# Moving pair 1's state products ahead of a weight tile, and thirteen small matmuls in place of one filler, in an SSD and PReLU kernel on TensorE

## The chip, the cores and the metric

The kernel runs on one core of one Trainium2 chip. The metric is the device time in microseconds (us) of one execution. Times inside an execution are counted from the start of the span, which runs from the first to the last instruction that the profile shows.

## The reference

Two stages follow each other. The first is a state-space recurrence (Mamba 2) over 4 batches, 8 heads, 768 positions, head dimension 32 and state size 16, by chunks:

```python
cum = np.cumsum(la, axis=-1)
L = np.exp(cum[:, :, :, None] - cum[:, :, None, :]) * causal
M = np.einsum('bhin,bhjn->bhij', Cc, Bc) * L
y_intra = np.einsum('bhij,bhjd->bhid', M, xc)
y_inter = np.einsum('bhin,bhnd->bhid', Cc, state) * decay_to_i[:, :, :, None]
y[:, :, sl] = y_intra + y_inter
state = decay_full[:, :, None, None] * state + np.sum(Bx, axis=2)
```

Its result, as 3072 tokens of 256 values, goes through a layer of 2048 hidden units with a PReLU of one slope per unit:

```python
h = x @ w_in                                   # 256 -> 2048
g = np.maximum(h, 0.0) + alpha * np.minimum(h, 0.0)
out = g @ w_out                                # 2048 -> 256
```

The two weights arrive as float64 and are made into float32 in the kernel.

## The kernel before, in words

**Staging.** The 3072 tokens are 24 chunks of 128, handled in pairs of chunks. Six groups of 512 tokens (two pairs each) go through the layer. For group 0 the layer is written out plainly: `hidden` (L1077) multiplies a 128-column piece of w_in with the group's 512 tokens, ScalarE (L1080) and VectorE (L1081) do the PReLU, and `output` (L1124) multiplies the result with a piece of w_out into four PSUM banks. Later groups use a scheme of seven products for eight (L1198, L1208, L1223, L1280) and take most of the time. The recurrence for a later pair is done in advance, in pieces between these products.

**Order.** Nothing is scheduled at run time: the order of the code is the order of the instructions on each engine. Each of TensorE, VectorE, ScalarE, GpSimd and SyncE (which issues the transfers) goes through its own list and waits for tiles by semaphores. PSUM is held in pools: `ss` and `hp` (two tiles each) and four `bank`s.

**Weights.** Pieces of 512 columns come as raw float64 halves (transfers issued at L254) and are turned to float32 by hand on three engines: ScalarE L270, L280 and L283, VectorE L293 and L305, GpSimd (or VectorE) L275, and last GpSimd L327, which adds the two parts into `w_in` or `w_out`. A matmul with such a piece waits for L327.

**The first two pairs.** `first_two` does pairs 0 and 1 by halves of 64 positions, and between the steps multiplies the first tokens with the first pieces of w_in (`hidden_two`: two pieces of w_in, each in two steps k, 256 tokens, PSUM tile handed in; matmuls at L1092). For one pair, the steps are:
- `turned`: transposes of B and C on TensorE (L838), copied out by ScalarE (L840)
- `spread`: 32 small matmuls (L858) that copy decays over partitions; VectorE scans them (L864)
- `spread_c`: ScalarE makes `cz` (L847)
- `added`: 16 matmuls of 64 x 32 tiles (L888), the chunks' additions to the state; `states` (L903, VectorE, three and then one) chains them; `one_at_a_time` masks the states on GpSimd (L909)
- `gram_of`: 16 matmuls (L874), and `times` (L880, VectorE) multiplies them with the scanned decays
- `x_products`: 32 matmuls (L922) and `state_products` (L934), which sum the output of the pair; ScalarE copies it out (L942, L943)

The change touches a filler behind `spread` of pair 1 and the place of `added` of pair 1. In the kernel before, `hidden_two` for the third and fourth piece of w_in is called with `among(i, k)`, which runs after each of its four matmuls: `added`, `states` and `one_at_a_time` after the first, `gram_of`, `times`, the last state and a PReLU after the second, and `x_products`, `state_products` and `copy_out` after the third.

**Fillers.** `keep_warm(to, n, cols)` (L331 to L336) multiplies a constant tile of ones with itself into a PSUM tile that is not yet needed; its result is read by nobody. It stands at several places of the first part.

**Later pairs.** From pair 2 on, `pair` does the same steps with full chunks (L624 the state products, L637 the states on VectorE, L562 the scans, L737 the gram, L748 its product with the decays). The decay factors that L637 needs come by two transfers: `pf<-rpf` (L442) writes them out, `ap<-pf` (L167) brings them back spread over the partitions.

Of the kernel before, what the change touches and what calls it, by code (L numbers as in the profile page):

```python
# [22 lines left out]
def kernel(  # L23
# [25 lines left out]
    nc = tc.nc  # L49
# [7 lines left out]
    Q = 128  # L57
# [46 lines left out]
    def bank(i):  # L104


        return ps_q.tile([P, 512], F32, name="bank", tag=f"q{i}")
# [180 lines left out]
    def sign(dst, src, sg):  # L288

        if src.dtype == F32 or id(dst) in signs:  # L290
            return
        r = wtp.tile([P, 2, WQ], U32, name="wr")
        nc.vector.tensor_single_scalar(out=r, in_=parts[id(dst)][0], scalar=SIGN,  # L293
                                       op=ALU.bitwise_and)
        signs[id(dst)] = r
# [34 lines left out]
    warm = nc.const_aps.tensor(1.0, [P, 1], F32)  # L330

    def keep_warm(to, n, cols=2 * Q):

        for i in range(n):
            nc.tensor.matmul(to[:, :cols], warm.to_broadcast([P, P]), warm.to_broadcast([P, cols]),
                             start=True, stop=True, skip_group_check=True)  # L336
# [53 lines left out]
    def slope_signs():  # L390
        if moe_w_out.dtype == F32:
            nc.vector.tensor_single_scalar(out=s_out, in_=s_mul.bitcast(U32), scalar=SIGN,
                                           op=ALU.bitwise_and)
        else:
            for o, by in ((g_mul, 2.0**-11), (g_add, 2.0**25)):
                nc.gpsimd.tensor_scalar(out=o, in0=s_mul, scalar1=by, scalar2=None, op0=ALU.mult)
# [119 lines left out]
    def pair_loads(gp):  # L516

        b, c = divmod(2 * gp, CPB)
        nat, abc, xt, ap = loads["p", gp]

        bn = work.tile([P, 2, H * N], F32, name="bn")
        i, bi = divmod(b, 2)
        if gp >= HALF:
            pj = prt[i].rearrange("p (j b m h) -> p j b m h", j=2, b=2, h=H)[:, :, bi, c // 2]
        else:
            pj = (prt[i if gp >= NB else "short"]
                  .rearrange("p (b h c) -> p b c h", b=2, h=H)[:, bi, c : c + 2])
        nc.gpsimd.tensor_tensor(
            out=bn.rearrange("p k (h n) -> p k h n", h=H),
            in0=nat[:, 0].rearrange("p k (h n) -> p k h n", h=H),  # L530
            in1=pj.unsqueeze(3).to_broadcast([P, 2, H, N]), op=ALU.mult)
        return bn
# [8 lines left out]
    def spare():  # L541

        return ps_h.tile([P, GT], F32, name="hp", tag="hp")
# [272 lines left out]
    def first_two():  # L816
# [34 lines left out]
        def spread(z, ts):  # L851
            for e in range(2):
                for r in range(4):
                    rs = slice(32 * r, 32 * r + 32)
                    row = 32 * r + N * e
                    for j, hs in enumerate(halves):
                        o = ts[r][hs, : 2 * Q].rearrange("p (k e t) -> p k e t", k=2, e=2)
                        nc.tensor.matmul(o[:, :, e], ident[rs, row : row + 1]  # L858
                                         .to_broadcast([32, HQ]), z[rs, :, hs], start=e == 0,
                                         stop=True, tile_position=(32 * r, HQ * j),  # L860
                                         skip_group_check=True)
# [5 lines left out]
        def gram_of(bc, cz, banks):  # L867
            for v in range(2):
                for k in range(2):
                    for r in (2 * v, 2 * v + 1):  # L870
                        rs = slice(32 * r, 32 * r + 32)
                        for j, hs in enumerate(halves):
                            o = banks[r][hs, (2 + k) * Q : (3 + k) * Q]
                            nc.tensor.matmul(o.rearrange("p (e t) -> p e t", e=2), bc[rs, k, hs],  # L874
                                             cz[rs, :, k, hs], start=True, stop=True,
                                             tile_position=(32 * r, HQ * j),
                                             skip_group_check=True)

        def times(i, r, t):
            nc.vector.tensor_tensor(out=dec[i][:, r], in0=t[:, 2 * Q :], in1=dec[i][:, r],  # L880
                                    op=ALU.mult)

        def added(dps, bn, xt):
            for k in range(2):
                for r in range(4):
                    rs = slice(32 * r, 32 * r + 32)
                    for j, hs in enumerate(halves):
                        nc.tensor.matmul(dps[j][rs, k], bn[hs, k, rs],  # L888
                                         xt[hs, k, 2 * r * D : 2 * (r + 1) * D],
                                         start=True, stop=True, tile_position=(HQ * j, 32 * r),  # L890
                                         skip_group_check=True)

        def dps_in(banks):
            return [t[:, 2 * Q : 2 * Q + 4 * D].rearrange("p (k m) -> p k m", k=2) for t in banks]

        def states(i, dps, pf, cs=range(4)):
            for c in cs:
                if i == 0 and c == 0:
                    nc.scalar.copy(out=new[0][:, 0], in_=dps[0][:, 0])
                    continue  # L900
                e = (c + 1) * HQ - 1
                old = new[i][:, c - 1] if c else new[0][:, 3]
                nc.vector.scalar_tensor_tensor(out=new[i][:, c], in0=old, scalar=pf[:, e : e + 1],  # L903
                                               in1=dps[c % 2][:, c // 2], op0=ALU.mult,
                                               op1=ALU.add)

        def mask(i, cs):
            n = cs.stop - cs.start
            nc.gpsimd.tensor_tensor(  # L909
                out=sm[i][:, cs].rearrange("p k (g m) -> p k g m", g=2),  # L910
                in0=new[i][:, cs].unsqueeze(2).to_broadcast([P, n, 2, 2 * D]),
                in1=hmask.rearrange("p (g m) -> p g m", g=2).unsqueeze(1)
                .to_broadcast([P, n, 2, 2 * D]), op=ALU.mult)
# [31 lines left out]
        def places(first, second):  # L945
            return [[t[:, :Q].rearrange("p (k t) -> p k t", k=2) for t in ts]
                    for ts in (first, second)]
# [4 lines left out]
        def decayed_c(bc, pf):  # L952
            cd = work.tile([P, 2, Q], F32, name="cd")
            nc.gpsimd.tensor_tensor(out=cd.rearrange("p k t -> p (k t)"),
                                    in0=bc[:, 2:].rearrange("p k t -> p (k t)"), in1=pf,
                                    op=ALU.mult)
            return cd

        def one_at_a_time(i, cs):
            for c in cs:  # L960
                mask(i, slice(c, c + 1))
# [9 lines left out]
        sp = [bank(r) for r in range(4)]  # L971
# [5 lines left out]
        nat1, _, xt1, pf1 = loads["p", 1]  # L977
# [13 lines left out]
        dps = dps_in([hp, tp])  # L991
# [18 lines left out]
        sp = [bank(r) for r in range(4)]  # L1010
# [1 line left out]
        x_products(y, xt0, 0, (1,))  # L1012
        state_products(y, 0, cd0)
        spread(z1, sp)
        keep_warm(sp[3][:, 2 * Q :], 1)
        convert_next(halves=(nc.gpsimd, nc.gpsimd))
        xts[0] = xtp.tile([P, KC, GT], F32, name="xT")
        copy_out(0, y)
# [8 lines left out]
        bn1 = pair_loads(1)  # L1027
        convert_next(first=False)
        own = [ss(), ss()]
        second = spare()  # L1030
        bc1 = turned(nat1, (own[0], second))
        cz1 = spread_c(bc1)
        dps = dps_in(own)
        mask(0, slice(3, 4))
        slope_signs()
        cd1 = decayed_c(bc1, pf1)

        def among(i, k):
            if (i, k) == (0, 0):
                added(dps, bn1, xt1)  # L1040
                states(1, dps, pf1, range(3))
                one_at_a_time(1, range(3))
            if (i, k) == (0, 1):
                gram_of(bc1, cz1, sp)
                for r in range(4):
                    times(1, r, sp[r])
                states(1, dps, pf1, (3,))
                prelu_of[0]()
                convert_a(*pieces[2])
                sign(*pieces[2])  # L1050
            if (i, k) == (1, 0):
                y = places([own[0], bank(0)], [bank(1), bank(2)])
                x_products(y, xt1, 1)
                state_products(y, 1, cd1)
                copy_out(1, y)
# [349 lines left out]
    def convert_next(first=True, **kw):  # L1405


        i = done[0]
        if i < len(pieces):
            convert(*pieces[i], **kw)  # L1410
            if first and i and i + 2 < len(pieces):
                convert_a(*pieces[i + 2])
            if loaded[0] == i + 6:
                load_next()
        done[0] += 1
# [147 lines left out]
```

## Time and profile before

| what | value |
|---|---|
| times of three runs | 361.19, 361.89, 363.96 us (median 361.89) |
| the profiled execution's own time | 361.22 us |
| its span, from first to last instruction | 359.5 us |
| mean granted TensorE clock | 0.991 |
| instructions | 7769, of them 2981 matmuls and 2981 weight loads |
| half clock granted | up to 6.47 us, and from 23.54 to 30.36 us |
| VectorE, ScalarE, GpSimd busy | 67%, 48%, 56% of the span |
| data moved | 30.24 MB, mean 84 GB/s |

The span leaves out 1.7 us that lie before the first and after the last instruction. A float32 matmul stands in the trace as two passes with a weight load each, so a call of `nc.tensor.matmul` counts two in PE and two in PEld; a transpose counts one. In the timeline lines the columns are: start (us), length (us), engine, line, operation, what it writes and reads, the tile of the array, the shape, and how often it follows in a row; in brackets the idle time before it and what released it. The page also gives the share of 16 DMA engines that are moving data.

### The profile page before, as it was taken

How to read it: one execution, taken by the hardware profiler on the slowest of the kernel's cores; microseconds unless marked ns; L12 is line 12 of the kernel's file. 1: busy time of each engine (PE TensorE's matmuls, PEld its weight loads, DVE VectorE, ACT ScalarE, POOL GpSimd, SP SyncE). 2: the span in 40 equal slices, each digit the busy share in tenths (PEclk: the TensorE clock that was granted, in tenths of full speed). 3: DMA queues.
4: the chain of work that ended last, by engine and by line, in shares of the span. 5: the costliest groups of instructions: out<-in, count | busy, mean ns of one | idle time of the engine just before them, and what ended most of it. 6: DMA issues, size and time to landing. Idle time of an engine off the chain costs nothing.

```text
span 359.5 us, 7769 instructions
## 1 busy us (share of the span) xinstructions
PE 352.6 (98%) x2981; PEld 286.4 (80%) x2981; DVE 239.6 (67%) x483; ACT 172.3 (48%) x391; POOL 202.2 (56%) x227
## 2 busy tenths in 40 slices
PE   8889999999999999999999999999999999999996
PEld 3567566668888888888888888888888888888885
DVE  6966996999947856866656856657856634643363
ACT  3537666535354445445345445445545444443431
POOL 6653748579847947536546536537536545434510
PEclk9988999999999999999999999999999999999999
DMA  8999999205436502502522521531201001001102
GB/s 149 189 211 339 253 282 204 77 2 116 131 86 145 110 3 60 116 3 49 101 61 51 94 64 43 97 69 42 34 2 31 0 2 29 2 1 29 33 0 58
DMA packets 105581, 30.24 MB, mean 84 GB/s; under 512 B 79896, under 2 KB 101448, under 8 KB 105544
## 3 DMA queue, kind: packets, MB, share of 16 engines
q1 hardware_dynamic: 103048, 29.43, 35.6%
q10 hardware_dynamic: 2496, 0.32, 0.6%
q8 instruction: 23, 0.38, 0.4%
q14 instruction: 14, 0.11, 0.1%
HBM read 26.32 MB, written 3.42 MB: 83 GB/s over the span
## 4 chain that ended last, share of the span: by engine, by line
PE 96%; DMA 1%; DVE 1%; issue 0%; POOL 0%; SPq 0%; ACT 0%; POOLq 0%
PE bank L1198 33%; PE hp L1223 28%; PE bank L1124 8%; PE hp L1077 6%; PE ss L1223 6%; PE hp L1092 2%; PE ss L782 1%; PE ss L726 1%; DMA nat<-in_B_dram 1%; PE bank L1191 1%; PE ss L800 1%; PE ss L774 1%; PE ss L737 1%; PE bank L1092 1%; PE ss L613 1%; PE ss L934 0%
## 5 line engine op out<-in xcount | busy, mean ns | idle before, releaser
L1280 POOL TENSOR_TENSOR gt<-gt 128x512 f32<-128x512 f32 x58 | 74.2, 1278 | 21.1 <-DVE gt L1208 16.3
L1198 PE MATMUL bank<-gt,w_out 128*128 128x256 f32 x320 | 83.5, 381 | 0.0
L1198 PEld LDWEIGHTS bank<-gt,w_out 128*128 128x128 f32 x320 | 60.1, 190 | 9.2 <-issue 1.0
L1208 DVE SCALAR_TENSOR_TENSOR gt<-hp,s_mul,gt 128x256 f32<-128x256 f32 x96 | 42.0, 479 | 29.1 <-ACT gt L1206 26.8
L1270 POOL TENSOR_TENSOR gt<-gt 128x512 f32<-128x512 f32 x20 | 25.4, 1269 | 62.6 <-DVE gt L1208 49.8
L1206 ACT ACTIVATE gt<-hp,s_alpha 128x256 f32<-128x256 f32 x96 | 40.3, 471 | 34.6 <-PE hp L1223 31.5
L1198 PE MATMUL bank<-gt,ws 128*128 128x256 f32 x224 | 55.9, 379 | 0.0
L1198 PEld LDWEIGHTS bank<-gt,ws 128*128 128x128 f32 x224 | 42.3, 190 | 5.6
L1223 PE MATMUL hp<-xs,w_in 128*128 128x256 f32 x160 | 41.9, 384 | 0.0
L1223 PE MATMUL hp<-xs,ws 128*128 128x256 f32 x160 | 41.2, 380 | 0.0
L1249 DVE TENSOR_TENSOR hp<-hp,u 128x512 f32<-128x512 f32 x20 | 14.0, 700 | 35.2 <-ACT u L1247 35.2
L1223 PEld LDWEIGHTS hp<-xs,ws 128*128 128x128 f32 x160 | 30.3, 190 | 4.3 <-POOL xs L1165 0.2
L1223 PEld LDWEIGHTS hp<-xs,w_in 128*128 128x128 f32 x160 | 29.7, 190 | 4.5
L1124 PE MATMUL bank<-w_out,gt 128*128 128x256 f32 x128 | 31.0, 384 | 0.0
L1124 PEld LDWEIGHTS bank<-w_out,gt 128*128 128x128 f32 x128 | 23.6, 190 | 6.5 <-issue 2.9
L1223 PE MATMUL ss<-xT,w_in 128*128 128x256 f32 x96 | 24.6, 379 | 0.0
L1077 PE MATMUL hp<-xT,w_in 128*128 128x512 f32 x48 | 22.7, 595 | 0.0
L556 DVE TENSOR_TENSOR_SCAN dec<-abc,bank 128x192 f32<-128x192 f32 x48 | 22.7, 523 | 0.0
L640 POOL TENSOR_TENSOR sm<-state,bmask 128x256 f32<-128x256 f32 (+1 forms) x10 | 6.2, 619 | 28.9 <-DVE state L637 28.9
L1238 ACT COPY m<-hp 128x512 f32<-128x512 f32 x8 | 4.7, 586 | 35.7 <-PE hp L1223 35.7
L1247 ACT COPY u<-hp 128x512 f32<-128x512 f32 x20 | 11.7, 585 | 19.4 <-PE hp L1223 19.4
L1208 DVE SCALAR_TENSOR_TENSOR gt<-c,s_mul,gt 128x256 f32<-128x256 f32 x40 | 20.6, 555 | 0.0
(230 smaller groups left out, 615.8 us busy)
## 6 DMA issues: line engine op xcount, KB each, us to landing
abc<-z SPq DMA_DIRECT2D x24, 192.0 KB
raw<-in_moe_w_in_dram SPq DMA_DIRECT2D x8, 512.0 KB
raw<-in_moe_w_out_dram SPq DMA_DIRECT2D x8, 512.0 KB
abc<-z SPq DMA_DIRECT2D x8, 512.0 KB
out_dram<-o_sb SPq DMA_DIRECT2D x32, 64.0 KB
nat<-in_B_dram SPq DMA_DIRECT2D x26, 64.0 KB
xt<-in_x_dram SPq DMA_DIRECT2D x12, 128.0 KB
xt<-in_x_dram SPq DMA_DIRECT2D x24, 64.0 KB
```

What stands on the lines that cost most here:

```text
L556: nc.vector.tensor_tensor_scan(out=dv[:, o : o + SQ], data0=abc[k][:, s : s + SQ], data1=ident_p[0][:, :SQ], initial=0.0, op0=ALU.mult, op ...
L1077: nc.tensor.matmul(hp, w_in[:, k, f * P : (f + 1) * P], xts[g][:, k], start=(k == 0), stop=(k == KC - 1))
L1092: nc.tensor.matmul(hp[:, i * nt : (i + 1) * nt], w_in[:, k, fs], xts[g][:, k, ts], start=(i == 0 and k == 0), stop=(k == KC - 1), skip_gro ...
L1124: nc.tensor.matmul(pos[0][t // 2][:, t % 2], gt[:, t * Q : (t + 1) * Q], w_out[:, f], start=(f == 0 and t % 2 == 0), stop=(f == NF - 1), s ...
L1198: nc.tensor.matmul(ms[g][i][:, h], w, blocks[g, z][n][:, p], start=(q == 0 and h == 0), stop=(q == NQ - 1), skip_group_check=True)
L1206: nc.scalar.mul(o[:, p], h[:, p], s_alpha[:, fs[p]])
L1208: nc.vector.scalar_tensor_tensor(out=o[:, p], in0=h[:, p], scalar=s_mul[:, fs[p]], in1=o[:, p], op0=ALU.mult, op1=ALU.max)
L1223: nc.tensor.matmul(to[:, p], w(2 * z + p), b, start=start and p == 0, stop=True, skip_group_check=True)
L1247: nc.scalar.copy(out=u2, in_=A)
L1249: nc.vector.tensor_tensor(out=Y, in0=Y, in1=u2, op=ALU.add)
L1270: nc.gpsimd.tensor_tensor(out=tc_, in0=g22, in1=g12, op=ALU.subtract)
L1280: eng.tensor_tensor(out=o, in0=x0, in1=x1, op=ALU.subtract)
```

## The change

It has two parts.

1. Behind `spread` of pair 1, the filler of one matmul of 128 x 128 with 256 columns is replaced by thirteen matmuls of 32 x 32 with 32 columns, of the same constant, on the corner tile of the array (position 0, 0), into the same PSUM bank.
2. `added`, `states` and `one_at_a_time` of pair 1 leave `among(0, 0)` and are issued in front of the call of `hidden_two` for the third piece of w_in; behind them comes a new filler of 256 columns into `second`, the PSUM tile that this `hidden_two` is about to use.

```diff
         spread(z1, sp)
-        keep_warm(sp[3][:, 2 * Q :], 1)
+        small = sp[3][:32, 2 * Q : 2 * Q + 32]
+        for i in range(13):
+            nc.tensor.matmul(small, warm[:32].to_broadcast([32, 32]),
+                             warm[:32].to_broadcast([32, 32]), start=True, stop=True,
+                             tile_position=(0, 0), skip_group_check=True)
         convert_next(halves=(nc.gpsimd, nc.gpsimd))
...
         cd1 = decayed_c(bc1, pf1)
+        added(dps, bn1, xt1)
+        states(1, dps, pf1, range(3))
+        one_at_a_time(1, range(3))
+        keep_warm(second, 1)
 
         def among(i, k):
-            if (i, k) == (0, 0):
-                added(dps, bn1, xt1)
-                states(1, dps, pf1, range(3))
-                one_at_a_time(1, range(3))
             if (i, k) == (0, 1):
                 gram_of(bc1, cz1, sp)
```

On VectorE, ScalarE, GpSimd and SyncE the instructions keep their order; only TensorE's list changes. Lines behind the change are four further on in the kernel after (L1092 becomes L1096, L1077 becomes L1081, L1081 becomes L1085, L1124 becomes L1128).

## The prediction

> **What bounds the kernel now.** I began with the page's busy times and its chain of work, then read the windows view in steps of 3.41 us (the rhythm of the granted clock), TensorE's timeline around the edit, and last VectorE, GpSimd and the transfers up to 50 us.
>
> ```profile
> PE 352.6 (98%) x2981; PEld 286.4 (80%) x2981; DVE 239.6 (67%) x483; ACT 172.3 (48%) x391; POOL 202.2 (56%) x227
> PE 96%; DMA 1%; DVE 1%; issue 0%; POOL 0%; SPq 0%; ACT 0%; POOLq 0%
> q8 instruction: 23, 0.38, 0.4%
> ```
>
> TensorE is the bound: 352.6 of 359.5 us. Only its few holes, or time at a reduced clock, can be won. Its last two holes lie where the edit is made:
>
> ```profile
> 13.37 0.70 PE L335 MATMUL bank<-const-float32-1.0 128*128 128x256 f32 x2
> ...
> 17.87 0.70 PE L1092 MATMUL hp<-xT,w_in 128*128 128x256 f32 x2 [1.20 <-POOL w_in L327]
> 18.50 0.46 PE L888 MATMUL ss<-xt,bn 64*32 64x64 f32 x32
> 18.89 0.70 PE L1092 MATMUL hp<-xT,w_in 128*128 128x256 f32 x2
> 19.52 0.72 PE L874 MATMUL bank<-cz,bc 32*64 32x128 f32 x32
> ...
> 23.05 0.41 PE L922 MATMUL bank<-dec,xt 64*32 64x64 f32 x20 [1.05 <-issue]
> ...
> 25.19 0.79 PE L1092 MATMUL hp<-xT,w_in 128*128 128x256 f32 x1
> ```
>
> The reader should see two holes: 1.20 us for the third tile of w_in, which GpSimd finishes at 17.82, and 1.05 us in the middle of the x_products, released by nothing but "issue". The second I read as instructions not yet there. Matmul and weight load count 2 x 2981 = 5962 instructions, and queue q8 has 23 packets: some 260 each. The stall falls inside a row of equal matmuls that wait for nothing. In the packet records one such packet moves at 20.58-21.63, behind data on full queues, and TensorE goes on 1.4 us after it.
>
> ```profile
> 16.70:20.11 3.41, 2.24 (x68) 1.36 (x68) 2.31 (x6) 2.96 (x8) 3.28 (x7) 1.00 1.01 314
> 20.11:23.53 3.42, 2.35 (x79) 1.41 (x70) 3.21 (x9) 0.47 (x1) 1.28 (x3) 1.00 0.85 105
> 23.53:26.94 3.41, 3.41 (x20) 3.02 (x21) 1.98 (x4) 1.36 (x6) 1.92 (x2) 0.50 1.04 253
> 26.94:30.35 3.41, 3.41 (x9) 2.69 (x9) 2.19 (x4) 2.41 (x6) 1.19 (x2) 0.50 0.92 293
> ```
>
> Columns: stretch, length, busy time of PE, PEld, DVE, ACT, POOL, the granted clock, the DMA share, GB/s. After the window of 20.11, full of tiny matmuls and holding the hole, the clock is halved for two windows: 6.83 us, in which 3.41 us of work is lost. From 25.19 on TensorE has no hole to the end.
>
> **What the Trainium skill says.** "Runtime: NRT & Kernel Launch", section Instruction fetch mechanics: the sequencer fetches blocks of 256 instructions by its own DMA queue, a cost it calls "mostly hidden". The trace agrees on the block (23 packets) and disagrees once on hidden (1.05 us). "TensorE: Matmul & The Clock Gate", Part 1: activity in a free-running window of 3413 ns releases the throttle, an idle window restores it. The trace shows the steps (23.54 to 30.36 is 2 x 3.41), but here a window with 2.35 of 3.42 us marked busy was followed by half speed, so what counts must be use of the array, not "busy".
>
> **The change part by part.** Each matmul stands in the trace as two passes with two weight loads.
> 1. Out: one filler of 256 columns, 13.37 to 13.98: 0.61. In: 13 x 2 passes of 32 x 32. Nearest row: passes of 64 columns on one tile (L922) every 56 ns. Half that for half the columns, or no less than that: 26 x 28 = 0.73 to 26 x 56 = 1.46. I take 0.75, so +0.14 (range +0.1 to +0.85). What follows, L1092 at 13.98, stops for GpSimd's L327, which ends at 14.62, then come the transposes L838 and the 1.20 hole: 0.14 is free. At +0.85 up to 0.45 would reach the copies of ScalarE (L840, 17.08 and 17.35) that free the PSUM for added.
> 2. Count: 12 more matmuls here, one filler more later: 13 x 4 = 52 more instructions ahead of the x_products (48 by the first L1092 of the third tile). They draw the request for the next block forward, from between 14.4 and 16.4, when the DMA share is 1.00, to about 13, where the packet records are at 0.14-0.38. Then it is there well before 21.
> 3. Added products (L888, 16 matmuls, 32 passes) before the third tile. They wait for xt (landing 16.24 and 17.07), bn, and ScalarE's second copy (17.35): 17.38 + 0.39 = 17.77. That is inside the hole of 1.20. The filler takes 2 x 0.2135 = 0.43: 18.20. The four passes of L1092 take 0.85 and 0.2 for the turn of the tiling: 19.25 for the gram (19.52 before), so -0.25. No DMA, VectorE, ScalarE or GpSimd instruction changes its place in a queue; VectorE's states (L903, 19.13 to 20.11) get their operand 1.1 earlier, with scans before them to 18.17.
> 4. x_products start 0.25 earlier and lose the 1.05 hole: last one ends 22.1 for 23.46; state_products at full clock take 1.0 for 1.80: 23.1 at most and 22.5 at best for the next L1092 (25.19 before), -2.1 to -2.7.
> 5. The clock. The window from 20.11 now holds some 1 us of full-array L1092 more at its end (22.5 to 23.53), and in the window before it the filler. I take it that it stays up: +3.41 of work. Together up to 2.1 + 3.41 = 5.5 us ahead by 30.36; the low end is 1.2 (hole and order alone).
>
> That lead does not last, which is the main step. VectorE waits at 39.26 for a transfer that TensorE does not drive:
>
> ```profile
> 34.01 0.60 SPq L167 DMA_DIRECT2D ap<-pf  x1
> ```
> ```profile
> 39.26 0.28 DVE L637 SCALAR_TENSOR_TENSOR state<-gt,ap,ss 128x64 f32<-128x64 f32 x1 [0.16 <-DMA ap<-pf]
> 39.46 2.41 DVE L562 TENSOR_TENSOR_SCAN dec<-abc,bank 128x256 f32<-128x256 f32 x4
> ...
> 47.29 0.69 DVE L305 SCALAR_TENSOR_TENSOR wr<-wt,wr 128x512 uint32<-128x512 uint32 x1
> ```
> ```profile
> 48.07 1.27 POOL L327 TENSOR_TENSOR w_out<-wr,wg 128x512 uint32<-128x512 uint32 x1 [1.16 <-DVE wr L305]
> ```
> ```profile
> 49.48 0.39 PE L1124 MATMUL bank<-w_out,gt 128*128 128x256 f32 x1
> ```
>
> ap is issued at 34.01 because pf lands at 34.00 after its issue at 27.00, behind weight tiles in queues at a share near or above 1.0 from 22 on; it lands at 39.17. Behind L637 VectorE works without a hole to 47.98 (scans, two conversions, two activations), GpSimd sums the third piece of w_out from 48.07 to 49.34, and TensorE's L1124 needs that at 49.48. Slack: 0.14. However early TensorE is at 39, it starts that L1124 at 49.34 or later, and from there to the end it is full. So the gain is at most 0.14, or some 0.5 if the transfers begin a little earlier (the share of 0.85 in the window of 20.11 leaves 0.15 x 3.42 = 0.5).
>
> What is late next: TensorE, 4 to 5 us ahead, reaches pair 2's gram (L737) near 39.2 and waits for VectorE's L1081, which ends at 43.65. It stands idle about 4.4 us across the window 40.60-44.01 (the 3.41 grid continued). If the clock is halved at 44.01, the rest up to 49.48, 4.5 us of full-speed work after 43.65 (gram 1.1, two L1124 and L1077 3.5), does not fit: 43.65 to 44.01 does 0.36, the window to 47.43 1.7, the remaining 2.4 ends at 49.87 if the clock comes back: +0.4. With a second half window: 1.7 by 50.84, then 0.7 more, against 47.43 + 2.4: 51.55, so +2.1; part of it is given back where the lead is smaller. Sum for the likeliest case, against the profiled 361.22: -0.1 for the slack, +0.4 for one late half window, weighed with none: 361.2 to 361.6. The median of three runs is 361.89, 0.67 above the profiled run, so the next median may lie there too. I take 361.6.
>
> **The rivals.**
> A (likeliest, 0.57): the holes and most of the early half speed go, the lead is given back at ap; 361.2 to 362.0.
> B (0.24): the change doesn't do what it says: the stall moves to other instructions or the clock is halved all the same. For: how full a window must be is seen here in one case only, and a window a little more or less full decides. TensorE then still meets the wait at 49.34 with what it had: 361.0 to 361.9, no change either.
> C, slower (0.13): the idle stretch at 39 to 44 halves the clock for two windows or more at 44.01 and VectorE, waiting for late products, carries it on: 361.22 + 2.1 = 363.3, with both windows fully at half 361.22 + 3.4 = 364.6, and past 365.5 only with a third. It decides from a lead of about 3.4 us, which empties a whole window. For: at 23.53 the clock was halved after a window less empty than this one, and for two windows. Against: the windows before and after this one are full, unlike then.
> D, faster (0.06): ap is not the wall, because pf or the weight tiles come earlier: 361.2 - 4.9 = 356.3, half kept 358.8. Against: the slack of 0.14 is read directly.
>
> **How the numbers follow.** A and B are both within 1% (3.6 us, about what a measurement of this kernel can tell from no change: 358.3 to 365.5), most of C too. Faster: 0.05 from D. Slower: 0.05 from C's end and from the small tiles costing more than bounded. Same 0.90. Range: A and B reach 361.0 to 362.0, C to 363.8, D's partial gain to 360.5: 360.5 to 363.8.
>
> **What would show it.** No "issue" in front of L922 and x_products starting near 20.5 (steps 2, 3); windows 23.53 and 26.94 at 1.00 (step 5); L1077's first run near 26 to 27; ap landing within 0.5 of 39.17; a TensorE hole of 4 us released by VectorE before the gram L737; L1124 of the third piece within 0.2 of 49.34, or later with a clock of 0.50 from 44.01 (C). Wrong, if ap lands over 1 us earlier, if TensorE keeps a lead past 50, or if clock steps appear after 50.

## The result, and the profile after

The changed kernel took 362.90 us (median of 20 runs, 361.34 to 369.42), the kernel before 362.17 us (20 runs, 360.26 to 364.23): ratio 1.0021, 95% interval 0.9997 to 1.0045. An execution more than 1.5% above the fastest of its kernel, such as the one of 369.42, is left out of this ratio and of those below. That is no difference that this measurement can tell, or a small loss. The forecast was 361.6 (range 360.5 to 363.8) and no change.

The profiled execution of the changed kernel took 362.82 us, its span 361.1. From its page, the busy times and the chain by engine:

```profile
PE 352.7 (98%) x3007; PEld 287.9 (80%) x3007; DVE 238.3 (66%) x483; ACT 172.0 (48%) x391; POOL 202.9 (56%) x227
PE 91%; DMA 5%; DVE 3%; issue 1%; SPq 0%; ACT 0%; DVEq 0%
```

TensorE's work is the same, but the chain that ends last no longer runs over TensorE alone: 5% of it are now transfers and 3% VectorE. The chain between 25 and 53 us names them (start, length, what):

```profile
27.99 7.70 DMA pf<-rpf
35.70 0.02 issue
35.71 4.62 DMA ap<-pf
...
40.42 0.28 DVE state L637
40.70 2.33 DVE dec L562 x4
```

TensorE's timeline, and VectorE's and GpSimd's at the same place:

```profile
13.31 0.27 PE L1017 MATMUL bank<-const-float32-1.0 32*32 32x32 f32 x3
14.34 0.95 PE L1017 MATMUL bank<-const-float32-1.0 32*32 32x32 f32 x23 [0.75 <-issue]
...
20.03 0.46 PE L888 MATMUL ss<-xt,bn 64*32 64x64 f32 x32 [0.78 <-issue]
20.41 0.70 PE L335 MATMUL hp<-const-float32-1.0 128*128 128x256 f32 x2
...
44.86 0.48 PE L737 MATMUL hp<-cz,bc 32*128 32x256 f32 x1 [1.55 <-DVE gt L1085]
...
51.11 1.24 PE L1128 MATMUL bank<-w_out,gt 128*128 128x256 f32 x5
```
```profile
40.42 0.28 DVE L637 SCALAR_TENSOR_TENSOR state<-gt,ap,ss 128x64 f32<-128x64 f32 x1 [3.40 <-DMA ap<-pf]
```
```profile
48.99 1.27 POOL L327 TENSOR_TENSOR w_out<-wr,wg 128x512 uint32<-128x512 uint32 x1 [2.04 <-DVE wr L305]
```

Before, VectorE waited 0.16 us for ap; now it waits 3.40: TensorE's lead, turned into idle time of VectorE, and later into 1.55 us of TensorE's own in front of pair 2's gram. ap came 1.16 us later than before (L637 at 40.42 for 39.26), because its source was late: L439, which VectorE runs behind products of TensorE, before and after:

```profile
24.14 1.42 DVE L439 TENSOR_TENSOR_SCAN rpf<-r,zeros 96x128 f32<-96x128 f32 x1
```
```profile
26.53 1.43 DVE L439 TENSOR_TENSOR_SCAN rpf<-r,zeros 96x128 f32<-96x128 f32 x1
```

The windows view, on the 3.41 us grid of this execution (columns as before):

```profile
11.65:15.07 3.42, 2.67 (x94) 2.23 (x90) 3.14 (x8) 1.95 (x6) 2.12 (x3) 1.00 0.70 77
15.07:18.48 3.41, 3.41 (x14) 2.72 (x12) 2.86 (x5) 0.00 (x0) 2.24 (x5) 0.50 0.96 235
...
42.38:45.79 3.41, 1.86 (x17) 0.99 (x16) 3.31 (x7) 1.80 (x3) 1.65 (x3) 1.00 0.77 125
45.79:49.20 3.41, 3.41 (x9) 2.58 (x9) 3.31 (x7) 0.00 (x0) 1.29 (x3) 0.50 1.06 190
```

Two windows are at half speed, but others than before: one behind the hole in the small matmuls, one behind the idle time at the gram. The steps of the clock lie at other times too: before at 23.54, here at 15.07, and 8.47 between them is no multiple of 3.41. The grid has its own phase in each execution.

The sum of this execution: GpSimd begins the third piece of w_out 0.92 later (L327 at 48.99 for 48.07). TensorE, behind the half window, uses it only 0.85 after it is ready (ready at 50.26, used at 51.11); before that was 0.14. 0.92 + 0.85 - 0.14 = 1.63. The span grew by 1.6.

### The profile page after: what moved, and what is told of

It reads as the page before. It is cut to its first block, busy times and chain, and to the rows that moved or that the text cites. A ratio compares the mean times of both kernels' runs of the same rounds, so it can differ in the third digit from the quotient of the medians.

```text
span 361.1 us, 7820 instructions
## 1 busy us (share of the span) xinstructions
PE 352.7 (98%) x3007; PEld 287.9 (80%) x3007; DVE 238.3 (66%) x483; ACT 172.0 (48%) x391; POOL 202.9 (56%) x227
## 3 DMA queue, kind: packets, MB, share of 16 engines
HBM read 26.32 MB, written 3.42 MB: 82 GB/s over the span
## 4 chain that ended last, share of the span: by engine, by line
PE 91%; DMA 5%; DVE 3%; issue 1%; SPq 0%; ACT 0%; DVEq 0%
PE bank L1202 33%; PE hp L1227 28%; PE bank L1128 7%; PE ss L1227 6%; PE hp L1081 4%; DMA pf<-rpf 2%; PE ss L782 1%; DMA ap<-pf 1%; PE ss L726 1%; PE hp L1096 1%; DMA nat<-in_B_dram 1%; PE bank L1195 1%; PE ss L800 1%; PE ss L774 1%; PE ss L737 1%; DVE dec L562 1%
## 5 line engine op out<-in xcount | busy, mean ns | idle before, releaser
L1210 ACT ACTIVATE gt<-hp,s_alpha 128x256 f32<-128x256 f32 x96 | 40.3, 471 | 34.6 <-PE hp L1227 31.5
L1128 PE MATMUL bank<-w_out,gt 128*128 128x256 f32 x128 | 32.6, 399 | 0.0
L1128 PEld LDWEIGHTS bank<-w_out,gt 128*128 128x128 f32 x128 | 24.8, 199 | 6.8 <-issue 3.7
L1081 PE MATMUL hp<-xT,w_in 128*128 128x512 f32 x48 | 22.6, 594 | 0.0
```

The costliest lines, as they stand in the source:

```text
L1081: nc.tensor.matmul(hp, w_in[:, k, f * P : (f + 1) * P], xts[g][:, k], start=(k == 0), stop=(k == KC - 1))
L1128: nc.tensor.matmul(pos[0][t // 2][:, t % 2], gt[:, t * Q : (t + 1) * Q], w_out[:, f], start=(f == 0 and t % 2 == 0), stop=(f == NF - 1), s ...
L1210: nc.scalar.mul(o[:, p], h[:, p], s_alpha[:, fs[p]])
```

## The experiments

All times are medians over 14 to 22 runs beside the kernel before on the same chip. Where a kernel has fillers or small matmuls more or less than the changed one, only products that nobody reads are concerned.

**The parts alone, both together, and the idle time filled.** The small matmuls without the move:

```diff
-        keep_warm(sp[3][:, 2 * Q :], 1)
+        small = sp[3][:32, 2 * Q : 2 * Q + 32]
+        for i in range(13):
+            nc.tensor.matmul(small, ...)
```

> Only the thirteen small matmuls; the added products stay behind the first matmul of the third tile. Theory 1 (the wall: what TensorE does before 40 counts only where it delays VectorE's L439 and so pf and ap; a hole of instructions in the small matmuls empties the clock window there and a half clock at about 15 makes everything late): the hole of 0.7 to 0.9 us stands inside the small matmuls, half speed in one window near 15 to 18.5 where the phase is as in the profile after, ap lands 0.5 to 1.1 us later than 39.17, and the time is 0 to 1 us over before. Theory 2 (the moved products are what costs): time as before within 0.2 us. Theory 3 (fetch of instructions decides: the hole at the x_products goes, and 1 us is won): 1 us under before.

Measured: 361.80, ratio 0.9999 (0.9979 to 1.0020). That is theory 2's time, and the lower end of theory 1's. Theory 1's hole and half window did not come: in the profile the small matmuls have no hole, but the one at the x_products is there, 1.45 us, and no window after 5.3 us is at half speed. But for the hole that execution is what the forecast wanted for TensorE, and it took 360.95 us: 0.27 less than the profiled one of before, which lost 3.41 us of work at half speed. The lead is gone at L637, in VectorE's timeline:

```profile
39.14 0.28 DVE L637 SCALAR_TENSOR_TENSOR state<-gt,ap,ss 128x64 f32<-128x64 f32 x1 [3.57 <-DMA ap<-pf]
```

The move without the small matmuls:

```diff
-        for i in range(13):
-            nc.tensor.matmul(small, ...)
+        keep_warm(sp[3][:, 2 * Q :], 1)
```

> Only the move of the added products with its filler; the filler of 256 columns stays behind spread. Theory 1: no hole of instructions behind spread, the added products run inside the wait for w_in near 17.4, the x_products begin near 20.5; the hole of 1.05 us in front of the x_products stays nearly where it was, since only 4 more instructions come first; TensorE is up to 0.5 us earlier at 30 and this is given back at the wait for ap; time as before within 0.3 us. Theory 2 (the move costs): 0.4 to 0.8 us over before. Theory 3: as before, since the hole stays.

Measured: 362.07, ratio 0.9992 (0.9970 to 1.0013). Its profile has the hole at the x_products at 1.62 us and one half window from 25.06. Theory 1's time holds, and theory 2's loss did not come; theory 1's 17.4 for the added products does not hold (18.11): TensorE had waited 0.54 and 0.21 us for pieces of w_in in front of the transposes.

The filler kept in front of the small matmuls, with the move:

```diff
+        keep_warm(sp[3][:, 2 * Q :], 1)
         for i in range(13):
             nc.tensor.matmul(small, ...)
```

> The kernel after with the filler of 256 columns kept in front of the thirteen small matmuls. Theory 1: the block of instructions is now asked for later by 0.6 us than in the kernel after, the hole in the small matmuls shrinks from 0.94 to 0.3 us or less, the window is fuller and the half clock near 15 comes seldom; 0.3 to 0.8 us faster than after, near before. Theory 2 (the move costs): as after. Theory 3 (more instructions early pay): 1 us under before.

Measured: 363.11, ratio 1.0032 (1.0007 to 1.0057). The hole in the small matmuls did shrink to 0.18, and the clock was full from 5.56 to 46.52. But the hole at the x_products was 1.18, and TensorE was idle for 2.15 us at the gram, with a half window behind it (46.52 to 49.94). The expected gain did not come: in this execution a full clock early was paid for later.

The changed kernel with fillers in the idle time before the gram:

```diff
             gram = {r: ss_tile() if r < small else spare() for r in range(4)}
+            if gp == 2:
+                keep_warm(gram[0], 2, GT)
```

> The kernel after with two fillers of 512 columns (1.7 us at full clock) in front of pair 2's gram, where TensorE is idle for 1.9 us in the profile after. Theory 1: they cost nothing, since that time waits for VectorE, and they hold the clock up: no half speed near 45 to 49, 0.5 to 0.9 us faster than after. If no lead is there in most executions, they delay the gram's last row by up to 1.7 us and the time rises by about as much. Rival: idle time there has nothing to do with the later half clock; the time stays as after.

Measured: 362.56, ratio 1.0010 (0.9991 to 1.0028), between before and after, and its interval holds both. The profiled execution, the slowest of its 22, had its half windows early (23.54 to 30.37) and ap late (issued at 37.30). The fillers ran from 45.14 to 46.95, and VectorE's activation for which the gram waits ended at 46.81: so they stood in time that would have been idle, some 1.0 us by an estimate (the first half of the gram takes 0.7 us), and no late half window followed. One such execution does not show that they prevented one. Inconclusive on the clock.

**Taking the wall away.** pf and ap of pair 2 issued by ScalarE, whose queue holds no weight tiles, in the kernel after, in the kernel before, and with the small matmuls alone:

```diff
-        nc.sync.dma_start(out=scratch["pf", 0], in_=rpf)
+        nc.scalar.dma_start(out=scratch["pf", 0], in_=rpf)
...
-    load_products(NB, loads["p", NB][3])
+    load_products(NB, loads["p", NB][3], nc.scalar)
```

> The kernel after, but pf is written out and pair 2's ap read back by transfers that ScalarE issues (a queue of their own), not behind the weight tiles in SyncE's queue. Theory 1 (ap is the wall that takes the lead back): ap lands several us before 39, L637 no longer waits for it, SyncE is not held until pf lands, and the first product with the third piece of w_out (49.5 to 52.3 in the five profiles so far) starts 1 to 3 us earlier; the time falls by as much, to 360 or less, and then depends on the half clock before 40, in steps of up to 3.4 us. Rival (the weights themselves, bound by the transfers, are the wall, and ap only happens to land with them): ap lands earlier and the time stays within 0.5 us of after. Second rival: ScalarE, held until pf lands, delays the conversions, 0.5 us or more slower.

> The same edit in the kernel before. Theory 1: with the half clock and the hole of 1.05 us before 30 no longer hidden, before gains less than after does: 0 to 1 us, and its time spreads more with the mean clock than it did. Rival (weights are the wall): no change, or the same gain in both kernels.

> The thirteen small matmuls alone, with the same edit of the queues. Theory 1: without the hole at the x_products and with the added products in their old place this has the earliest TensorE of all, and the wall no longer hides it: fastest of the three, 1 to 3 us under before. Rival: as before.

Measured: 362.88, ratio 1.0013 (0.9995 to 1.0031); 361.76, 0.9994 (0.9975 to 1.0014); 362.70, 1.0014 (0.9994 to 1.0033). By the medians nothing is won. The profiled executions, one of each kernel, show two cases. In that of the changed kernel, the fastest of its 22, ap was there in time. VectorE's and TensorE's timelines:

```profile
37.31 0.27 DVE L637 SCALAR_TENSOR_TENSOR state<-gt,ap,ss 128x64 f32<-128x64 f32 x1
```
```profile
47.19 1.99 PE L1128 MATMUL bank<-w_out,gt 128*128 128x256 f32 x8 [0.43 <-POOL w_out L327]
```

L637 waits for nothing, the third piece of w_out is used 3.92 us earlier than in the profile after, and the execution took 359.63 us for 362.82, with the clock full from 4.97 us to the last microsecond of its span. In those of before and of the small matmuls alone pf took 6.3 and 6.9 us even in a queue of its own, and ScalarE, which must wait for it before it issues ap, stood for 3.95 and 4.54 us. ScalarE's timeline with the small matmuls alone:

```profile
33.56 1.18 ACTq L167 DMA_DIRECT2D ap<-pf  x1
34.79 0.84 ACT L1106 ACTIVATE gt<-bank,s_alpha 128x256 f32<-128x256 f32 x2 [4.54 <-issue]
```

VectorE and TensorE then were late themselves, and L637 began at 41.21 and 41.81 without a wait for ap. So two of the three profiles show the second rival, ScalarE held, and one shows theory 1: in those two, removing one wait put another in its place. How often each happens is not known.

The same with the small matmuls alone, ap issued by ScalarE later, behind the first hidden piece of the loop:

```diff
         hidden(0, f)
+        if f == FIRST:
+            load_products(NB, loads["p", NB][3], nc.scalar)
```

> The thirteen small matmuls alone, pf and ap by ScalarE's queue as in the three runs before, but ap is issued by ScalarE after the first hidden piece of the loop, four activations later, so that ScalarE does not stand until pf has landed (4.5 us in the profile of the thirteen alone with the early ap). Theory 1: no wait of ScalarE over 1 us there, ap lands before VectorE reaches L637, the first product with the third piece of w_out starts near 47 to 48 when the clock is full: 358.5 to 360.5, faster than before by 1.5 to 3. Rival (the weight tiles themselves come too late): as before within 0.5 us.

Measured: 361.46, ratio 0.9982 (0.9962 to 1.0002). The lowest median of all, yet the interval still touches 1, and it is far from the 1.5 to 3 us expected. In its profile ScalarE no longer stood, as theory 1 said, but ap did not land in time: L637 still waited for it, 0.93 us, to 39.86. pf had landed at 30.40. ap was issued at 33.64, when ScalarE came to it behind its other work, and took 6.13 us. So 3.2 us went to the new place of ap, and this run does not show what an early ap is worth.

**Why the changed kernel looks a little slower.** The small matmuls behind the transposes, directly in front of the added products:

```diff
-        for i in range(13):
-            nc.tensor.matmul(small, ...)
...
+        for i in range(13):
+            nc.tensor.matmul(small, ...)
         added(dps, bn1, xt1)
```

> The kernel after with the thirteen small matmuls behind the transposes, directly in front of the added products, where TensorE waits for ScalarE's copies. Theory 1 (each part alone costs nothing and both together about 0.9 us, because the small matmuls delay the transposes and the moved products put ScalarE's copies of these on the path of the third tile): the transposes end at 16.5 or earlier, the added products start near 17.4, and the time is that of before within 0.3 us, 0.6 to 1 us under after. Rival (the loss has nothing to do with the transposes): as after.

Measured: 361.61, ratio 1.0001 (0.9981 to 1.0021), as theory 1 said. But the profile, of the slowest of its 14 executions, does not support its reason: the last transposes began at 17.04 and the added products at 19.45, for the small matmuls in front of them stood 1.09 us, to 18.52, behind VectorE's scan (L864) of the PSUM bank into which they write. The edit brought in a wait of its own, so it does not test the theory's reason. The clock was full until 46.97, TensorE stood 3.38 us at the gram, and that execution took 363.95 us.

Twice as many small matmuls, in the changed kernel and without the move, and the changed kernel again:

```diff
-        for i in range(13):
+        for i in range(26):
```

> The kernel after with 26 small matmuls for 13: some 0.8 us more in front of the transposes (a pass took 31.5 ns). Theory 1 (small matmuls in front of the transposes cost only together with the moved products, which put ScalarE's copies of the transposes on the path of the third tile): transposes, copies, added products and pf's issue are 0.5 to 0.8 us later than in after, and so is the first product with the third piece of w_out; time 0.4 to 0.8 us over after. Rival (the loss of after is the moved products' own and the small matmuls are free): as after.

> 26 small matmuls alone, with the added products in their old place. Theory 1: the added products there start about 1.1 us after ScalarE's second copy, so 0.8 us more is hidden: within 0.3 us of the kernel with 13 alone and of before. Rival (small matmuls cost what they take, wherever the products stand): 0.5 to 0.8 us over before, as much over before as the 26 add to after.

> The kernel after once more, beside the other three on one chip. Theory 1: 0.4 to 1.0 us over before, at a mean clock of 1.00 too (362.2 against 361.2 so far). Rival (the first 20 runs of after were only unlucky in the phase of the clock): within 0.2 us of before.

Measured: 363.20, ratio 1.0027 (1.0004 to 1.0051); 362.84, 1.0031 (1.0009 to 1.0053); 362.20, 1.0012 (0.9990 to 1.0035). Twenty-six cost the same with the move and without it, 0.9 us by the median of the latter, near the rival's 0.5 to 0.8. The theory that the two parts cost only together falls for twenty-six; for thirteen these times do not decide it. The changed kernel again, 0.25 us over before, lies between its theory (0.4 to 1.0) and its rival (0.2). The two measurements of the changed kernel, taken as independent, average to 1.0016, from 1.0000 to 1.0033: a loss near 0.6 us is likely, and not shown.

A possible cause of it stands in the profiles. With the move, and pf in SyncE's queue, pf was issued at 27.79 to 28.59 (seven executions); without it at 26.43 to 27.00 (before, small alone, 26 alone). In the profile after VectorE's L439, which makes pf's source, ended only at 27.96 (25.56 before); in the second one it ended at 26.10, but SyncE came to pf only at 28.55, behind its weight tiles. Against it: the move alone shows no loss (0.9992), and 26 alone shows one without a late issue. It stays open.

These profiles bear on two other points. First, the hole of the instructions. The changed kernel again, and with 26 small matmuls in place of 13 and no move:

```profile
23.87 0.26 PE L922 MATMUL bank<-dec,xt 64*32 64x64 f32 x1 [1.99 <-issue]
```
```profile
21.68 0.88 PE L922 MATMUL bank<-dec,xt 64*32 64x64 f32 x33
```

With 13 the hole at the x_products is not gone: 1.99 us. With 26 it is, in both kernels; there the packet of instructions moved at 15.06 and 15.99, not at 20.93 and 21.63 as in the two executions of the changed kernel with 13. Second, the clock: here the lead was paid for by half speed. The windows view of the 26 alone:

```profile
37.13:40.54 3.41, 3.41 (x13) 2.08 (x11) 0.00 (x0) 2.26 (x4) 0.00 (x0) 1.00 0.93 307
40.54:43.96 3.42, 1.33 (x7) 0.59 (x6) 3.02 (x7) 1.80 (x3) 1.76 (x3) 1.00 0.94 227
43.96:47.37 3.41, 2.09 (x11) 1.27 (x11) 3.41 (x6) 0.00 (x0) 2.49 (x3) 0.50 0.80 99
47.37:50.78 3.41, 3.41 (x8) 2.77 (x9) 3.31 (x7) 0.00 (x0) 1.28 (x2) 0.50 0.95 246
```

TensorE is earliest of all here, VectorE does nothing from 37.13 to 40.54 but wait for ap, TensorE then stands 3.41 us at the gram, and two windows follow at half speed: what the forecast's rival C described.

All fourteen profiled executions in one table. "Used at" is the start of the first product with the third piece of w_out; times in us from the start of the span:

| kernel | ap issued | L637 began | idle at the gram | half speed between 12 and 55 | used at | used - L637 | span - used |
|---|---|---|---|---|---|---|---|
| before | 34.01 | 39.26 | 0 | 23.54-30.36 | 49.48 | 10.22 | 310.0 |
| after | 35.71 | 40.42 | 1.55 | 15.07-18.48, 45.79-49.20 | 51.11 | 10.69 | 310.0 |
| after, again | 35.68 | 41.08 | 0 | 23.46-30.29 | 50.97 | 9.89 | 310.1 |
| small alone | 33.74 | 39.14 | 1.55 | none | 49.04 | 9.90 | 310.2 |
| move alone | 35.87 | 41.16 | 0.66 | 25.06-28.47 | 51.05 | 9.89 | 310.1 |
| filler and small, move | 35.44 | 40.61 | 2.15 | 46.52-49.94 | 51.35 | 10.74 | 310.0 |
| after, gram filled | 37.30 | 42.43 | 0 | 23.54-30.37 | 52.33 | 9.90 | 310.3 |
| after, own queue | 29.04 | 37.31 | 0 | none | 47.19 | 9.88 | 310.1 |
| before, own queue | 32.96 | 41.21 | 0 | 38.40-41.82 | 51.10 | 9.89 | 310.1 |
| small alone, own queue | 33.56 | 41.81 | 0 | 38.28-41.70 | 51.70 | 9.89 | 310.2 |
| small behind transposes | 36.12 | 41.68 | 3.38 | 46.97-50.38 | 52.37 | 10.69 | 309.9 |
| after with 26 | 35.71 | 41.31 | 2.77 | 44.75-51.58 | 53.18 | 11.87 | 309.9 |
| 26 alone | 35.77 | 40.84 | 3.41 | 43.96-50.78 | 52.54 | 11.70 | 309.9 |
| small alone, own queue, ap later | 33.64 | 39.86 | 0 | 22.70-29.52 | 49.76 | 9.90 | 310.1 |

Whatever was done in front, the span is the moment of that product plus 309.9 to 310.3. That moment in turn follows VectorE's L637. GpSimd's L327 of the third piece began 8.56 to 8.58 us behind L637 in thirteen executions, and the product 9.88 to 9.90 us behind it in the eight of these without a half window at 44 to 52; the five with one took 10.69 to 11.87. (Before, where TensorE had no lead, L327 came 8.81 us behind.) L637 waited for ap in eleven of the fourteen, in all but the first three with a queue of its own. So in these executions the edits show in the start of L637 or in a late half window. Early half windows count only as far as they move these: small alone with no half speed at all is 0.44 ahead of before with two early windows of it.

Two warnings. Each line is one execution, and some are no typical ones: those of the gram filled, of before with its own queue and of the small matmuls behind the transposes are the slowest of their runs. And over many runs the time does go with the clock: 208 runs of the kernel before, beside the experiments, have medians of 361.09 us at a mean clock above 0.997 (44 runs), 361.98 at 0.994 to 0.997 (75), 362.14 at 0.989 to 0.993 (80) and 364.13 below that (9). Where in those runs the half windows lay is not known.

## Why the prediction was right, and where its steps were not

**The main step held**: a lead of TensorE before 39 us ends at the wait for ap, and from the third piece of w_out on the kernel runs as it did. VectorE's wait grew from 0.16 to 3.40 us, and the constant steps from L637 to the third piece and from there to the end show the rest. Removing the wait was tried too, but only single executions gained by it, no median.

**What it held fixed.** The forecast let ap land within 0.5 us of 39.17. It landed at 40.33 in the profile after and at 40.98 in the second one, and that made the third piece 0.92 and 1.58 us later. Most of its other signs failed too in the profile after: the first run of L1081 (L1077 before) began at 29.55, not at 26 to 27, and the hole before the gram was 1.55 us, not 4. The lead that was to be lost was 2.26 us at the first L1128 (31.73 for 33.99), not up to 5.5, and in the second execution there was none (34.68). From profile to profile the time grew by 1.6 us, where the sum said 0 to 0.4. That the median came out inside the range was helped by how alike the rivals' times were: A, B and most of C all meant no change.

**The size.** The sum was made against 361.22, but over 20 runs the kernel before has a median of 362.17, so that execution was 0.95 below it, and not 0.67. With that the forecast's no change would have read 362.2 to 362.6; measured 362.90.

**Step 1** (small matmuls): a pass took 31.5 ns, 26 passes 0.82 us, near the low end of 0.73 to 1.46. The price taken from L922 was rough: its passes lie in groups of four, 25 to 152 ns from group to group, not 56 throughout. Missed was a hole of 0.75 and 0.55 us inside the small matmuls, in both executions of the changed kernel. A packet of instructions that landed at 12.82 was used at 14.34. With the small matmuls alone, and no hole, it had landed at 12.20. Before it landed at 12.30, and TensorE went on behind the filler at 13.98 without a wait.

**Step 2 failed**: "They draw the request for the next block forward". The next packet moved at 20.93 and 21.63 for 20.58 before, and the hole at the x_products stayed (1.99) or was only hidden by TensorE being late. In the executions where I could read such a hole, TensorE went on 1.28 to 1.48 us after the packet's end (eight of them). Twenty-six small matmuls brought the packet forward in both executions with them, but in three others (before and small alone with their own queue, small behind the transposes) it came at 15.5 to 16.8 without. So the number of instructions is not the whole cause; what decides it stays open. Full queues do not tell the two kinds apart: the DMA share from 14 to 20 us is 0.92 to 1.04 in all fourteen.

**Step 3**: the order was right, the price was not. The added products wait for ScalarE's second copy, as said, but started at 20.03 and 18.17 (17.62 in the kernel after with its own queue), not at 17.38, because the transposes ended late: behind the hole in both executions, behind half speed in the first. With the move alone and neither of them it was 18.11, because w_in came late. The forecast held 17.35 fixed, though part 1 and w_in stand in front of it.

**Step 4** follows from these: the x_products began at 23.19 and 21.33 for 20.55 forecast, in the second case with the hole inside them.

**Step 5 failed as put** ("I take it that it stays up"). The windows at 23.53 and 26.94 stayed up in the profile after, but the clock's windows lie differently in each execution. In the profile after the early half window came before the x_products, in the second one exactly where it had been before (23.46 to 30.29). The 1.55 us of idle time at the gram show what the phase does: with the small matmuls alone it lies across the end of a window (42.85, from steps at 5.30 and every 3.413) and nothing follows; in the changed kernel it lies inside one, 42.38 to 45.79, and the next is at half speed.

The forecast's reading that use of the array counts, not "busy", can be put to the test with all fourteen traces. An estimate of use: each pass counts by its share of the 128 x 128 array and by its columns, at 216 ns for 256 of them (the spacing of L1124's passes before). Cut into its own windows of 3.413 us, up to 75 us, an execution then shows when half speed follows:

| use in a window | at full speed | half speed follows | at half speed | half speed follows |
|---|---|---|---|---|
| up to 1.18 us | 13 | 13 | 6 | 6 |
| 1.20 to 1.27 us | 6 | 3 | 0 | |
| above 1.36 us | 239 | 0 | 16 | 0 |

Busy time does not divide them: 2.35 us (before, at 20.11) and 2.67 us (after, at 11.65) were followed by half speed, and 2.24 us (before, at 16.70) was not. In use these are 0.92, 0.88 and 1.51 us. Part 1 lowers it: the filler that it takes out is 0.43 us of use, its 26 passes of 32 x 32 are 0.04 us. So the change took use from the window at 11.65, behind which the clock was at half speed in the profile after.

**Rival C**, the later half window, was the case in the profile after, at the price of 0.85 (0.4 forecast for one window). It needs no lead of 3.4 us; 1.55 us of idle time were enough. It goes with the main step: of six executions with no half window between 20 and 38 and pf in SyncE's queue, five have one at 44 to 52, and the sixth is the lucky phase above. The five with a half window at 22 to 31 have none late (one of them with the gram filled, one with ap later). In these executions early speed was exchanged for late speed.

**Rival D** (a lead kept) did not happen, but the changed kernel with its own queue shows that it was no fancy: one execution with ap in time and a full clock took 359.63, the fastest of its 22; the median was 362.88.

The Trainium skill, "TensorE: Matmul & The Clock Gate", Part 1, gives the window's 3413 ns and says that it does not restart with the kernel; the steps at other phases agree. By the page the throttle comes back after an idle window; here windows in which TensorE was busy for 2.67, 1.86 and 1.33 us of 3.41 were enough.

## What to carry to other kernels

Follow a stall to be removed to the next wait that its engine's consumers have on something else, and read the slack there: here 0.14 us at one weight tile. Of the fourteen executions only two used that tile earlier than before, one by 0.44 us and one, with ap in time, by 2.29. A lead that cannot be used becomes idle time, and idle time inside one clock window can halve the clock in the next, as can a window of small matmuls that use little of the array. One profiled execution is one phase of that clock: judge edits that move a clock window or a packet of instructions by several profiles.

## What was not expected of the hardware

The granted clock was half behind windows with TensorE busy 78% of the time (2.67 of 3.42 us, tiny matmuls and a hole). By the estimate above what divides the windows is the use of the array: at most 1.18 us of 3.41 where half speed always followed, at least 1.36 where it never did, and the same for whether one half window or two followed. A packet of instructions (16 KB) was used only 1.3 to 1.5 us after its transfer had ended. A transfer of 48 KB (pf) took 6.9 us in a queue of its own, for 7.0 to 7.7 in SyncE's queue behind weight tiles in before and after, while another execution had it in 3.5 or less. The DMA share from 25.5 to 29 us was 0.88 in the slow case and 0.94 in the quick one, so the share does not explain it, and the cause stays open.
